# Strassen-style expert layers on one core: the first block's second layer takes the other token half first, later blocks keep totals

## The chip, the cores and the metric

The kernel runs on one core of one Trainium2 chip. The metric is the device time of one execution in microseconds (us).

## The reference, cut to what matters

```python
def _attn_ref(q, k, v):            # 4 x 8 heads, 576 tokens, head 64
    ...                            # top-32 softmax attention
def _moe_ref(x, w1, w2, w3, w_out):
    a = x @ w1
    b = x @ w2
    return (a * b @ w3) @ w_out
def _moe2_ref(x, w_gate, w1, w2):  # N = 2304 tokens, D = 512, E = 8, F = 1024
    logits = x @ w_gate
    P = np.exp(logits - logits.max())
    for _ in range(8):             # rows, then columns, are normed
        ...
    for e in range(E):
        h = np.maximum(x @ w1[e], 0.0)
        out += P[:, e:e + 1] * (h @ w2[e])
    return out
```

The three follow each other. The change touches only the last one, `_moe2_ref`.

## The kernel before, in words

**Number format.** Every fp32 operand of a product is split into a high part in TensorE's fp32r format (ScalarE writes it) and a low part, which is the operand less its high part (VectorE or GpSimd subtracts). A product is then three matmuls: high by high, high by low, low by high.

**Blocks and units.** The expert layer takes 768 tokens (`TB`) at a time, so it has three blocks, s = 0, 1, 2. In a block it walks through 32 units (`NW`), n = 4e + u: expert e and a quarter u of the 1024 hidden columns (two slices of 128). The first layer of a unit is a 2 by 2 Winograd product: seven passes (functions `i0` to `i6`, in the order `CH` of products 6, 1, 4, 2, 0, 3, 5). A pass is a call of `prod`: six matmuls of 384 columns at L1141 into a PSUM bank (A, B or C of the unit; the pool has four), and behind it the sums that Winograd's scheme wants (VectorE, L1156, L1159, or L1352 in the later blocks). All engines work through the program's order, each its own instructions in turn.

**Block 0.** The function `l1` returns the seven passes. Its `relu(i, h, src)` writes for hidden slice i and token half h the high part `hh` (ScalarE, L1163) and right behind it the low part `hl` (VectorE, L1164, which needs the high part). The calls are (0,0) in pass 2, (1,1) in pass 4, (1,0) in pass 5 and (0,1) in pass 6, so half 0 is whole after pass 5 and half 1 after pass 6. The second layer is not Winograd: `l2(n, i)` makes token tile i (0 to 2 in half 0, 3 to 5 in half 1) with six matmuls of 512 columns at L1197 into one of three banks, and VectorE adds it to `acc` (L1208; L1204 for the first expert). The main loop puts one `l2` of the unit before behind each of the passes 1 to 6:

```python
for i, fn in enumerate(ops):
    fn()
    if n and i:
        l2(n - 1, (i + 2) % NTB)
```

so tiles come in the order 3, 4, 5, 0, 1, 2. Behind that the slot splits a weight tile of the next unit (`w_split`: ScalarE L966, GpSimd L967), makes a sum of weights of the unit after it (`w_sums`, VectorE L956, in passes 3 to 6), and takes a step of side work from a list (`slot`: first the norming of P, later the tokens of blocks 2 and 1). In pass 3 the second layer's weights are split (`w2_split`, GpSimd L983). On even u, `w2_more` also makes the seven Winograd weights of the second layer and keeps them in DRAM for the later blocks (VectorE L1001, ScalarE L1005, GpSimd L1006).

**Blocks 1 and 2.** Here the second layer is Winograd too, and it is fed by the gated hidden `h`, of which `d1` writes seven combinations (`parts`: high on ScalarE L1358, low on VectorE or GpSimd L1359). For a pair of units, `group(pair, k, j)` makes product k for output half j with six matmuls of 384 columns at L1413 in one of the three banks `yps`, and `add_m` adds it to an accumulator `M[k]` (VectorE L1423; in a block's first pair ScalarE copies, L1421). One group stands behind each pass, 14 for a pair. The weights of product k are fetched (`v_fetch`, L1317) or, for odd units of block 1, made from the raw weights `wr` (`v_make`: VectorE L1331, ScalarE L1333, GpSimd L1334).

**A block's end.** The scheme's totals are sums of the products. The table `early` puts ten sums of accumulators into the last two units (`plus`, L1427, VectorE and GpSimd), and `finish` runs the last pair's 14 groups in three chains: a chain keeps its PSUM bank and adds the next product to it, and VectorE reads it between (L1461, L1463). `out_cols` transposes the totals (L1433), copies them and sends them to DRAM (L1445, L1449). Block 1's end is followed by block 2's start, block 2's by nothing.

Of the kernel before, what the change touches and what calls it, by code (L numbers as in the profile page):

```python
# [7 lines left out]
F32 = mybir.dt.float32  # L8
# [4 lines left out]
AF = mybir.ActivationFunctionType  # L13
ALU = mybir.AluOpType
# [4 lines left out]
def kernel(  # L19
# [897 lines left out]
    NW = E * NU  # L917
    NP = NTB * (NSB - 1)
    CH = (6, 1, 4, 2, 0, 3, 5)
    KO = (1, 2, 3, 5, 7, 6, 4)  # L920
    V, G_ = nc.vector, nc.gpsimd
    pT = dram.tile([E, NP, 128], F32, name="pT")
    xk = {c: dram.tile([128, 2, KH, TH], F32, name=f"xk{c}") for c in CH}
# [200 lines left out]
    hs = {}  # L1124
    bn = {}
    ready_ps = {}

    def prod(n, c, bank, first):

# [16 lines left out]
    def l1(n):  # L1146

        t = {}

        def new(nm, shape, dt):  # L1150
            t[nm] = wp.tile(shape, dt, name=nm, tag=nm, bufs=2 if dt == F32R else 1)
            return t[nm]

        def plus(nm, ps, x):
            new(nm, [128, TH], F32)
            nc.vector.tensor_tensor(t[nm], ps, t[x], ALU.add)  # L1156

        def into(ps, x):
            nc.vector.tensor_tensor(ps, ps, t[x], ALU.add)  # L1159
            return ps  # L1160

        def relu(i, h, src):
            nc.scalar.activation(t["hh"][:, i, h], src, AF.Relu)  # L1163
            nc.vector.scalar_tensor_tensor(t["hl"][:, i, h], src, 0.0, t["hh"][:, i, h].bitcast(F32),  # L1164
                                           op0=ALU.max, op1=ALU.subtract)

        def i0():
            new("hh", [128, 2, 2, TH], F32R)
            new("hl", [128, 2, 2, TH], F32R)
# [89 lines left out]
    for n in range(NW):  # L1259
        e, u = units[n][1:]  # L1260
        ops = l1(n)
        nxt = units[n + 1][1:]
        nx2 = units[n + 2][1:]
        if n == 6:
            steps += x_ops(2) + p_steps() + x_ops(1)
        for i, fn in enumerate(ops):
            fn()
            if n and i:
                l2(n - 1, (i + 2) % NTB)
            (w_split if n + 1 < NW else w_fetch)(*nxt, CH[i])  # L1270
            if n + 2 < NW:
                if i == 0:
                    w_load(*nx2)
                if 3 <= i:
                    w_sums(*nx2, part=i - 3)
            if stores:
                stores.pop(0)()
            if more and i != 3:
                more.pop(0)()
            if i == 3:  # L1280
                w2_split(e, u)
                if n + 1 < NW:
# [40 lines left out]
    def v_make(n, k):  # L1323

        e, u = units[n][1:]
        a11, a12, a21, a22 = [wr[:, j, DH * i:DH * i + DH] for i in range(2) for j in range(2)]
        src = {1: a11, 2: a12, 3: a12, 5: wr5, 7: a21, 6: a11, 4: a22}[k]
        sums = {1: ((wr5, a21, a22, ALU.add), (a21, a11, a21, ALU.subtract)),
                2: ((a11, wr5, a11, ALU.subtract),), 3: ((a12, a12, a11, ALU.subtract),)}.get(k, ())
        for dst, x, y, op in sums:  # L1330
            nc.vector.tensor_tensor(dst, x, y, op)  # L1331
        t = wk2[n % 2][k]
        nc.scalar.activation(t[:, 0], src, AF.Copy)  # L1333
        nc.gpsimd.tensor_tensor(t[:, 1], src, t[:, 0].bitcast(F32), ALU.subtract)  # L1334
        keep2(e, u, k, t)

    def v_next(n, k):
        if n < len(units):
            (v_make if n < 2 * NW and n % 2 else v_fetch)(n, k)
            if k == KO[-1] and n % 2 and n + 2 < 2 * NW:  # L1340
                v_load(n + 2)

    def d1(n):

        last_ = (n + 1) % NW == 0
        e = units[n][1]
        h = hset[(n - NW) % 3]
        t = tmp
# [51 lines left out]
        return ([i0, i1, i2, i3, i4, i5, i6],  # L1400
                [j0, lambda: parts(7, t["t3"], G_), lambda: parts(6, t["t2"], V if last_ else G_),
                 lambda: parts(4, t["b21"], V if last_ else G_)])

    def group(pair, k, j, ps=None):

        again = ps is not None
        if not again:
            ps = yps.tile([128, 512], F32, name="y", tag="y")[:, 0:TH]
        q_ = 0
        for n in pair:  # L1410
            h, w = hset[(n - NW) % 3][k], wk2[n % 2][k]
            for a, b in ((0, 0), (0, 1), (1, 0)):
                nc.tensor.matmul(ps, w[:, a, 128 * j:128 * j + 128], h[:, b], start=(q_ == 0 and not again),  # L1413
                                 stop=(q_ == 5), skip_group_check=True)
                q_ += 1
        return ps

    def add_m(pair, k, j):
        ps = group(pair, k, j)
        if pair[0] % NW == 0:  # L1420
            nc.scalar.activation(M[k][:, j], ps, AF.Copy)  # L1421
        else:
            nc.vector.tensor_tensor(M[k][:, j], ps, M[k][:, j], ALU.add)  # L1423

    def plus(x, y, eng):
        for j in range(2):
            eng.tensor_tensor(M[x][:, j], M[x][:, j], M[y][:, j], ALU.add)  # L1427

    def out_cols(s, dh, th, j, y, st, eng=None):

# [20 lines left out]

    def finish(s, pair, late):

        bank = {}

        def run1(k, ch, j, *reads):
            bank[ch, j] = group(pair, k, j, bank.get((ch, j)))
            for x, op in reads:
                m = M[x][:, j]
                if op is None:  # L1460
                    V.tensor_tensor(m, m, bank[ch, j], ALU.subtract)  # L1461
                else:
                    V.tensor_tensor(m, bank[ch, j], m, ALU.add)  # L1463

        def run(k, ch, *reads):
            for j in range(2):
                run1(k, ch, j, *reads)

        run(1, "Z", (6, 1))
        late.pop(0)()  # L1470
        plus(7, 6, V)
        late.pop(0)()
        plus(3, 6, G_)
        run(2, "Z", (2, 1))
        for fn in late:
            fn()
        run(5, "Y", (7, 1))
        plus(4, 6, G_)
        run(3, "Y", (3, 1))
        o = [M[k] for k in (1, 5, 6, 2)]  # L1480
        for j in range(2):
            out_cols(s, 0, 0, j, M[2][:, j], o[0])
        run(7, "X", (3, None))
        run(6, "X", (7, 1), (3, 1))
        out_cols(s, 1, 1, 0, M[7][:, 0], o[1])
        run1(4, "X", 0, (4, 1))
        out_cols(s, 0, 1, 0, M[3][:, 0], o[2])
        out_cols(s, 1, 1, 1, M[7][:, 1], o[1])
        run1(4, "X", 1, (4, 1))
        out_cols(s, 0, 1, 1, M[3][:, 1], o[2])  # L1490
        out_cols(s, 1, 0, 0, M[4][:, 0], o[3], V)
        out_cols(s, 1, 0, 1, M[4][:, 1], o[3], V)

    early = {(-2, 6): (2, 1, G_), (-1, 0): (6, 1, G_), (-1, 1): (3, 5, V), (-1, 3): (4, 7, V), (-1, 4): (7, 5, V)}
    todo2 = []
    late = []
    p_load(1, 0)
    v_load(NW + 1)
    for n in range(NW, len(units)):
        s, e, u = units[n]  # L1500
        lone = n % NW < 2
# [5 lines left out]
        for i, fn in enumerate(ops):  # L1507
# [4 lines left out]
                w_fetch(*units[n + 1][1:], CH[i])  # L1512
            if todo2:
                pair, k, j = todo2.pop(0)
                add_m(pair, k, j)
                if j and pair[1] + 2 < NW * (s + 1):
                    v_next(pair[0] + 2, k)
                    v_next(pair[1] + 2, k)
            elif lone:
                v_next(n, KO[i])  # L1520
            if stores:
                stores.pop(0)()
            if late:
                late.pop(0)()
            x, y, eng = early.get(((n % NW) - NW, i), (0, 0, None))
            if x:
                plus(x, y, eng)
        late = later_
        if (n + 1) % NW == 0:
            finish(s, (n - 1, n), late)  # L1530
# [31 lines left out]
```

## Time and profile before

| | us |
|---|---|
| median of 3 runs | 2364.95 (2359.8 to 2366.29) |
| profiled execution, its time | 2366.93 |
| its span, first to last instruction | 2365.1 |
| block 0 from its first second-layer matmul to its last first-layer pass | 824.85 to 1367.82 |
| blocks 1 and 2, first pass of each | 1377.1 and 1873.6 |

| engine | busy us | share |
|---|---|---|
| TensorE matmul (PE) | 2226.4 | 94% |
| VectorE (DVE) | 1877.6 | 79% |
| GpSimd (POOL) | 1442.4 | 61% |
| ScalarE (ACT) | 1206.7 | 51% |

Matmuls overlap in the pipeline, so a busy PE is read by the distance between the starts of its matmuls and by its idle time. In a waiting row the number behind the name of the releaser is the wait's total, and then how often and the longest. Rows on the timeline give start, duration, engine, line, operation, what is written and read, and in brackets the engine's idle time before it and what ended that.

### The profile page before, as it was taken

What the parts mean: (1) busy time and instruction counts of PE and PEld (TensorE: products, weight loads), DVE (VectorE), ACT (ScalarE), POOL (GpSimd) and SP (SyncE); (2) the same over time, 40 slices, a digit from 0 to 9 for tenths busy, and PEclk for the clock granted to TensorE, in tenths of its full rate; (3) what the DMA queues carried; (4) which work ended last, traced back from release to release, by engine and by line L of the source; (5) the groups of instructions that cost most, each with busy time, mean ns of one, the idle gap of its engine ahead of it and who ended that gap; (6) DMA issues with size and microseconds to landing.
All of it is one profiled execution on the core that took longest, in us unless ns stands there. A gap on an engine that the chain in (4) does not pass through costs nothing.

```text
span 2365.1 us, 42495 instructions
## 1 busy us (share of the span) xinstructions
PE 2226.4 (94%) x13466; PEld 2032.9 (86%) x13466; DVE 1877.6 (79%) x4564; ACT 1206.7 (51%) x2706; POOL 1442.4 (61%) x1687
## 2 busy tenths in 40 slices
PE   5896999999999899999999989999999899999998
PEld 4555898889888787877788889999999899999997
DVE  8999899999995588877787766777777767777777
ACT  7999787787775334343333334443443343333332
POOL 6889776777764345565655546666666544444444
PEclk6997999999999999999999999999999999999999
DMA  6554444544541366686666687888888888787773
GB/s 186 151 148 117 105 113 100 124 108 109 124 97 46 121 214 219 223 291 227 237 230 225 222 278 265 277 274 273 274 277 268 297 280 260 252 260 256 255 258 120
DMA packets 350944, 482.57 MB, mean 204 GB/s; under 512 B 94881, under 2 KB 161025, under 8 KB 350721
## 3 DMA queue, kind: packets, MB, share of 16 engines
q1 hardware_dynamic: 349584, 478.03, 63.6%
q8 instruction: 108, 1.77, 0.3%
q10 hardware_dynamic: 1136, 1.84, 0.2%
q14 instruction: 116, 0.94, 0.1%
HBM read 306.59 MB, written 132.43 MB: 186 GB/s over the span
## 4 chain that ended last, share of the span: by engine, by line
PE 65%; DVE 14%; ACT 5%; POOL 5%; DMA 4%; issue 4%; SPq 2%; POOLq 0%; ACTq 0%; DVEq 0%
PE l1ps L1141 22%; PE y L1413 19%; PE abps L628 7%; PE y L1197 5%; PE x2ps L645 4%; PE sps L289 2%; DVE ws L956 2%; PE tx L427 2%; PE tx L398 2%; DVE hl L1164 1%; DVE tkv L338 1%; DMA ws<-in_moe_w_dram 1%; ACT hh L1163 1%; DVE acc L1208 1%; DVE l1ps L1159 1%
## 5 line engine op out<-in xcount | busy, mean ns | idle before, releaser
L1413 PE MATMUL y<-h,v 128*128 128x384 f32 x2688 | 551.0, 341 | 10.6 <-DVE M L1463 6.2
L1141 PE MATMUL l1ps<-xB,wa 128*128 128x384 f32 x2688 | 542.1, 338 | 9.0 <-DVE tm_u L1352 7.7
L1413 PEld LDWEIGHTS y<-h,v 128*128 128x128 f32 x2688 | 486.1, 190 | 12.5 <-DVE M L1463 7.4
L1141 PEld LDWEIGHTS l1ps<-xB,wa 128*128 128x128 f32 x2688 | 473.6, 188 | 13.6 <-DVE tm_u L1352 10.7
L967 POOL TENSOR_TENSOR wa<-ws,wa 128x256 fp32r<-128x256 f32 x217 | 169.1, 786 | 232.8 <-ACT wa L966 222.5
L1197 PE MATMUL y<-wb,hh 128*128 128x512 f32 x768 | 277.0, 403 | 32.2 <-ACT hh L1163 32.1
L1141 PE MATMUL l1ps<-xAh,wa 128*128 128x384 f32 x896 | 264.7, 342 | 4.1 <-DVE c L1156 2.0
L1359 POOL TENSOR_TENSOR h<-tm_t,h 128x384 fp32r<-128x384 f32 x188 | 192.0, 1031 | 89.7 <-ACT h L1358 85.9
L1423 DVE TENSOR_TENSOR M<-y,M 128x384 f32<-128x384 f32 x392 | 211.4, 551 | 40.8 <-PE y L1413 40.4
L1197 PEld LDWEIGHTS y<-wb,hh 128*128 128x128 f32 x768 | 147.0, 191 | 64.2 <-ACT hh L1163 39.8
L1359 POOL TENSOR_TENSOR h<-tm_b,h 128x384 fp32r<-128x384 f32 x126 | 133.4, 1064 | 97.9 <-ACT h L1358 84.1
L1358 ACT ACTIVATE h<-l1ps 128x384 fp32r<-128x384 f32 x128 | 63.0, 492 | 232.2 <-DVE l1ps L1355 232.2
L1141 PEld LDWEIGHTS l1ps<-xAh,wa 128*128 128x128 f32 x896 | 167.2, 191 | 14.7 <-DVE u L1156 3.9
L315 POOL TENSOR_TENSOR low<-s_sb 128x288 int32<-128x288 int32 x144 | 117.4, 815 | 99.5 <-ACT s_sb L293 97.4
L338 DVE MAX8 tkv<-rest 128x8 f32<-128x288 f32 x432 | 175.0, 446 | 0.0
L289 PE MATMUL sps<-kst,qst 128*128 128x288 f32 x640 | 130.0, 332 | 33.8 <-DVE top L322 31.9
L1197 PE MATMUL y<-wb,hl 128*128 128x512 f32 x384 | 156.5, 408 | 2.1
L1334 POOL TENSOR_TENSOR v<-wr,v 128x256 fp32r<-128x256 f32 x112 | 89.0, 797 | 113.2 <-ACT v L1333 89.8
L1141 PE MATMUL l1ps<-xAl,wa 128*128 128x384 f32 x448 | 151.8, 339 | 0.0
L289 PEld LDWEIGHTS sps<-kst,qst 128*128 128x128 f32 x640 | 100.0, 202 | 57.0 <-DVE top L322 45.4
L1208 DVE SCALAR_TENSOR_TENSOR acc<-y,P,acc 128x512 f32<-128x512 f32 x168 | 124.9, 744 | 23.5 <-PE y L1197 23.2
L1396 POOL TENSOR_TENSOR tm_t<-tm_b,tm_t 128x384 f32<-128x384 f32 x64 | 65.7, 1026 | 124.1 <-DVE tm_t L1392 119.9
(208 smaller groups left out, 5346.3 us busy)
## 6 DMA issues: line engine op xcount, KB each, us to landing
wa<-wk SPq DMA_DIRECT2D x448, 256.0 KB, 3.4
v<-vk SPq DMA_DIRECT2D x336, 256.0 KB, 3.7
wk<-wa SPq DMA_DIRECT2D x224, 256.0 KB, 2.6
vk<-v SPq DMA_DIRECT2D x112, 256.0 KB, 2.7
raw<-in_moe_w_dram SPq DMA_DIRECT2D x32, 512.0 KB, 3.8
ws<-in_moe_w_dram SPq DMA_DIRECT2D x128, 128.0 KB, 2.5
ws<-in_moe_w_dram SPq DMA_DIRECT2D x32, 512.0 KB, 4.5
vk<-sp SPq DMA_DIRECT2D x64, 256.0 KB, 3.1
```

What stands on the lines that cost most here:

```text
L289: nc.tensor.matmul(ps[:, e, 0:SH], lhs, kst[p, part][:, hh, SH * e:SH * e + SH], start=(n == 0), stop=(n == len(terms) - 1))
L315: nc.gpsimd.tensor_tensor(low_sb[st][:, j].bitcast(I32), x[:, 0:SH], x[:, SH:S], ALU.add)
L338: nc.vector.max(vt[:, j, c:c + 8], x[:, j])
L628: nc.tensor.matmul(ps[:, 0:n], lhs, rhs[:, c, 0:n], start=(m == 0), stop=(m == 3 * KD - 1))
L645: nc.tensor.matmul(ps[:, 0:n], W[:, f, 128 * c:128 * c + 128], G[:, f, 0:n], start=(f == 0), stop=(f == FC - 1))
L967: eng.tensor_tensor(t[:, 1], st[:, c], t[:, 0].bitcast(F32), ALU.subtract)
L1141: nc.tensor.matmul(ps, lhs[:, kc], rhs[:, kc], start=(first and k_ == 0), stop=(k_ == 3 * KH - 1), skip_group_check=True)
L1197: nc.tensor.matmul(ps, lhs[:, m, h, o:o + 128], rhs[:, m], start=(k_ == 0), stop=(k_ == 5))
L1208: nc.vector.scalar_tensor_tensor(a, ps, P[:, i, e:e + 1], a, op0=ALU.mult, op1=ALU.add)
L1359: eng.tensor_tensor(h[k][:, 1], src, h[k][:, 0].bitcast(F32), ALU.subtract)
L1413: nc.tensor.matmul(ps, w[:, a, 128 * j:128 * j + 128], h[:, b], start=(q_ == 0 and not again), stop=(q_ == 5), skip_group_check=True)
L1423: nc.vector.tensor_tensor(M[k][:, j], ps, M[k][:, j], ALU.add)
```

## The change

1. Block 0: the second layer takes tile i - 1 behind pass i (order 0 to 5).
2. Low parts made by VectorE (`hl`, and those of `parts(1)` and `parts(2)`) are put on a list and issued behind the slot's second-layer group, so behind VectorE's read of that group.
3. `w2_more` is also called for unit 1; block 1's unit 1 then fetches its weights, and the raw weights of its unit 3 are loaded before the block.
4. Blocks 1 and 2: products go in the order 1, 2, 5, 3, 7, 6, 4, and within a pair the chains Z (1, 2), Y (5, 3) and X (7, 6, 4) go on in their bank, so that `M[k]` holds a running total (M2 holds products 1 and 2, M3 holds 5 and 3, M6 holds 7 and 6, M4 holds 7, 6 and 4).
5. A block's end: the early sums are four, on GpSimd, `finish` has a new order with product 2 last, and the low parts there are made by GpSimd.
6. In `v_make` the weight sums move to products 2, 5 and 3.

```diff
-    KO = (1, 2, 3, 5, 7, 6, 4)
+    KO = (1, 2, 5, 3, 7, 6, 4)
+    CHAIN = {1: "Z", 2: "Z", 5: "Y", 3: "Y", 7: "X", 6: "X", 4: "X"}
...
+    after = []
+
+    def run_after():
+        while after:
+            after.pop(0)()
...
             nc.scalar.activation(t["hh"][:, i, h], src, AF.Relu)
-            nc.vector.scalar_tensor_tensor(t["hl"][:, i, h], src, 0.0, t["hh"][:, i, h].bitcast(F32),
-                                           op0=ALU.max, op1=ALU.subtract)
+            after.append(lambda: nc.vector.scalar_tensor_tensor(
+                t["hl"][:, i, h], src, 0.0, t["hh"][:, i, h].bitcast(F32), op0=ALU.max, op1=ALU.subtract))
...
-                l2(n - 1, (i + 2) % NTB)
+                l2(n - 1, i - 1)
+            run_after()
...
-                if u % 2 == 0:
+                if n % 2 == 0 or n == 1:
                     more = w2_more(e, u)
...
-        sums = {1: ((wr5, a21, a22, ALU.add), (a21, a11, a21, ALU.subtract)),
-                2: ((a11, wr5, a11, ALU.subtract),), 3: ((a12, a12, a11, ALU.subtract),)}.get(k, ())
+        sums = {2: ((wr5, a21, a22, ALU.add), (a21, a11, a21, ALU.subtract)),
+                5: ((a11, wr5, a11, ALU.subtract),), 3: ((a12, a12, a11, ALU.subtract),)}.get(k, ())
...
-            (v_make if n < 2 * NW and n % 2 else v_fetch)(n, k)
-            if k == KO[-1] and n % 2 and n + 2 < 2 * NW:
+            (v_make if NW + 1 < n < 2 * NW and n % 2 else v_fetch)(n, k)
+            if k == KO[-1] and n % 2 and NW + 1 < n < 2 * NW - 2:
                 v_load(n + 2)
...
-            eng.tensor_tensor(h[k][:, 1], src, h[k][:, 0].bitcast(F32), ALU.subtract)
+            low = lambda: eng.tensor_tensor(h[k][:, 1], src, h[k][:, 0].bitcast(F32), ALU.subtract)
+            (after.append if eng is V else lambda f: f())(low)
...
-            parts(5, t["t1"], V if last_ else G_)
+            parts(5, t["t1"], G_)
...
+    def group(pair, k, j, first=False):
+
+        first = first or k in (1, 5, 7)
+        if first:
+            bank[CHAIN[k], j] = yps.tile([128, 512], F32, name="y", tag="y")
+        ps = bank[CHAIN[k], j][:, 0:TH]
...
+    def take(pair, k, j, *dst, first=False):
+        ps = group(pair, k, j, first)
+        for x in dst:
+            m = M[abs(x)][:, j]
+            if x < 0:
+                nc.vector.tensor_tensor(m, m, ps, ALU.subtract)
+            elif pair[0] % NW == 0:
+                nc.scalar.activation(m, ps, AF.Copy)
+            else:
+                nc.vector.tensor_tensor(m, ps, m, ALU.add)
...
+        run(1, 1, 2)
         late.pop(0)()
         plus(3, 6, G_)
+        plus(5, 1, V)
+        run(5, 5)
         for fn in late:
             fn()
...
+        plus(3, 1, V)
+        run(3, 3)
+        plus(4, 1, V)
+        run(7, -3)
+        run(6, 5, 3)
+        out_cols(s, 1, 1, 0, M[5][:, 0], M[7])
+        take(pair, 4, 0, 4)
...
+        take(pair, 2, 0, 2, first=True)
+        out_cols(s, 1, 0, 1, M[4][:, 1], M[1])
+        take(pair, 2, 1, 2, first=True)
+        out_cols(s, 0, 0, 0, M[2][:, 0], M[5])
+        out_cols(s, 0, 0, 1, M[2][:, 1], M[5], V)
...
-    early = {(-2, 6): (2, 1, G_), (-1, 0): (6, 1, G_), (-1, 1): (3, 5, V), (-1, 3): (4, 7, V), (-1, 4): (7, 5, V)}
+    early = {3: (3, 7, G_, ALU.subtract), 5: (5, 6, G_, ALU.add)}
...
-    v_load(NW + 1)
+    v_load(NW + 3)
```

## Rows read from the trace of the kernel before

**Rows 1.** Busy time by stretch: length, engines' busy us, granted clock, DMA share.

```profile
1500.00:1600.00 100.00, 100.00 (x570) 99.73 (x569) 78.83 (x153) 41.41 (x94) 66.78 (x72) 1.00 0.80 272
1840.00:1885.00 45.00, 37.93 (x209) 35.50 (x207) 34.57 (x57) 12.70 (x28) 20.28 (x20) 0.96 0.78 294
2320.00:2365.00 45.00, 34.11 (x182) 32.24 (x180) 32.17 (x50) 8.52 (x19) 17.69 (x16) 0.90 0.27 83
```

**Rows 2.** Who waited for whom in block 0, 824 to 1377 us.

```profile
ACT hh L1163 <- DVE l1ps L1159: 139.2, 63, 3.7
DVE hl L1164 <- ACT hh L1163: 68.6, 117, 2.0
PE y L1197 <- ACT hh L1163: 32.1, 23, 3.6
```

**Rows 3.** Timeline at the turn from one unit of block 0 to the next.

```profile
1285.87 0.39 PE L1197 MATMUL y<-wb,hh 128*128 128x512 f32 x1
...
1287.26 0.34 PE L1141 MATMUL l1ps<-xAh,wa 128*128 128x384 f32 x1
...
1289.28 0.55 DVE L1159 TENSOR_TENSOR l1ps<-l1ps,u 128x384 f32<-128x384 f32 x1
1289.87 0.49 ACT L1163 ACTIVATE hh<-l1ps 128x384 fp32r<-128x384 f32 x1 [2.34 <-DVE l1ps L1159]
...
1290.41 0.50 PE L1197 MATMUL y<-wb,hh 128*128 128x512 f32 x1 [0.91 <-ACT hh L1163]
...
1290.86 0.48 ACT L1172 ACTIVATE p<-l1ps 128x384 f32<-128x384 f32 x1
```

**Rows 4.** Busy time in block 0: the first 11, next 10 and last 10 units.

```profile
824.85:1023.65 198.80, 182.87 (x858) 158.64 (x859) 167.84 (x292) 79.38 (x187) 114.61 (x122) 0.96 0.64 219
1023.65:1203.14 179.49, 164.99 (x782) 142.07 (x781) 141.10 (x221) 69.02 (x167) 109.17 (x116) 0.98 0.72 252
1203.14:1367.82 164.68, 159.62 (x780) 139.73 (x779) 129.45 (x207) 60.92 (x146) 87.69 (x95) 1.00 0.67 227
```

**Rows 5.** VectorE's groups in block 0, 830 to 1367 us: count, busy, mean ns, idle before.

```profile
L956 DVE TENSOR_TENSOR ws<-ws 128x256 f32<-128x256 f32 x116 | 112.3, 968 | 9.2 <-DMA ws<-in_moe_w_dram 7.2 <-POOL wb L983 1.9
L1001 DVE TENSOR_TENSOR sm<-ws 128x256 f32<-128x256 f32 x30 | 21.4, 715 | 0.0
```

**Rows 6.** Timeline of block 1's start.

```profile
1388.41 2.35 DVE L1331 TENSOR_TENSOR wr<-wr 128x256 f32<-128x256 f32 x2
...
1391.29 2.35 PE L1141 MATMUL l1ps<-xB,wa 128*128 128x384 f32 x12 [2.65 <-DVE tm_u L1352]
...
1407.39 1.43 DVE L1331 TENSOR_TENSOR wr<-wr 128x256 f32<-128x256 f32 x2 [6.80 <-DMA wr<-in_moe_w_dram]
...
1410.93 2.29 PE L1141 MATMUL l1ps<-xB,wa 128*128 128x384 f32 x6 [3.66 <-DVE tm_u L1352]
```

**Rows 7.** Timeline of block 2's start.

```profile
1885.53 5.60 PE L1141 MATMUL l1ps<-xB,wa 128*128 128x384 f32 x30 [0.37 <-DVE tm_u L1352]
```

**Rows 8.** Timeline of block 2's end.

```profile
2332.34 2.27 PE L1413 MATMUL y<-h,v 128*128 128x384 f32 x12
...
2336.65 1.34 PE L1413 MATMUL y<-h,v 128*128 128x384 f32 x6 [2.04 <-DVE M L1423]
...
2338.18 0.55 DVE L1393 TENSOR_TENSOR tm_t<-tm_b,l1ps 128x384 f32<-128x384 f32 x1
...
2340.82 2.63 DVE L1427 TENSOR_TENSOR M<-M,M 128x384 f32<-128x384 f32 x2
...
2358.65 0.52 PE L1433 MATMUL otp<-ident,M 128*128 128x128 f32 x3 [0.16 <-DVE M L1463]
...
2361.29 0.55 SPq L1449 DMA_DIRECT2D out_dram<-M  x1
```

**Rows 9.** Timeline of block 1 in its steady run: groups and VectorE's reads.

```profile
1506.02 1.22 PE L1413 MATMUL y<-h,v 128*128 128x384 f32 x6
...
1510.01 1.01 DVE L1423 TENSOR_TENSOR M<-y,M 128x384 f32<-128x384 f32 x2
```

More of the change, by code (lines that the diff above doesn't have):

```diff
@@ L1338, in v_next @@
         if n < len(units):
-            (v_make if n < 2 * NW and n % 2 else v_fetch)(n, k)
-            if k == KO[-1] and n % 2 and n + 2 < 2 * NW:
+            (v_make if NW + 1 < n < 2 * NW and n % 2 else v_fetch)(n, k)
+            if k == KO[-1] and n % 2 and NW + 1 < n < 2 * NW - 2:
                 v_load(n + 2)
     def d1(n):
-        last_ = (n + 1) % NW == 0
         e = units[n][1]
@@ L1397, in j0 @@
             G_.tensor_tensor(t["b21"], t["b21"], t["t2"], ALU.subtract)
-            parts(5, t["t1"], V if last_ else G_)
+            parts(5, t["t1"], G_)
         return ([i0, i1, i2, i3, i4, i5, i6],
[L1401 to L1408, printed above, removed]
+                [j0, lambda: parts(7, t["t3"], G_), lambda: parts(6, t["t2"], G_),
+                 lambda: parts(4, t["b21"], G_)])
+    bank = {}
+    def group(pair, k, j, first=False):
[3 more added lines that the diff above has]
+        ps = bank[CHAIN[k], j][:, 0:TH]
         q_ = 0
@@ L1412, in group @@
             for a, b in ((0, 0), (0, 1), (1, 0)):
-                nc.tensor.matmul(ps, w[:, a, 128 * j:128 * j + 128], h[:, b], start=(q_ == 0 and not again),
+                nc.tensor.matmul(ps, w[:, a, 128 * j:128 * j + 128], h[:, b], start=(first and q_ == 0),
                                  stop=(q_ == 5), skip_group_check=True)
@@ L1416, in group, with plus @@
         return ps
[L1418 to L1425, printed above, removed]
+    def take(pair, k, j, *dst, first=False):
[8 more added lines that the diff above has]
+                nc.vector.tensor_tensor(m, ps, m, ALU.add)
+    def plus(x, y, eng, op=ALU.add):
         for j in range(2):
-            eng.tensor_tensor(M[x][:, j], M[x][:, j], M[y][:, j], ALU.add)
+            eng.tensor_tensor(M[x][:, j], M[x][:, j], M[y][:, j], op)
     def out_cols(s, dh, th, j, y, st, eng=None):
@@ L1452, in finish, with run @@
     def finish(s, pair, late):
[L1454 to L1465, printed above, removed]
+        def run(k, *dst):
             for j in range(2):
[L1467 to L1471, printed above, removed]
+                take(pair, k, j, *dst)
+        run(1, 1, 2)
         late.pop(0)()
         plus(3, 6, G_)
-        run(2, "Z", (2, 1))
+        plus(5, 1, V)
+        run(5, 5)
         for fn in late:
             fn()
[L1477 to L1492, printed above, removed]
-    early = {(-2, 6): (2, 1, G_), (-1, 0): (6, 1, G_), (-1, 1): (3, 5, V), (-1, 3): (4, 7, V), (-1, 4): (7, 5, V)}
+        plus(3, 1, V)
[5 more added lines that the diff above has]
+        take(pair, 4, 0, 4)
+        out_cols(s, 0, 1, 0, M[3][:, 0], M[6])
+        out_cols(s, 1, 1, 1, M[5][:, 1], M[7])
+        take(pair, 4, 1, 4)
+        out_cols(s, 0, 1, 1, M[3][:, 1], M[6])
+        out_cols(s, 1, 0, 0, M[4][:, 0], M[1])
+        take(pair, 2, 0, 2, first=True)
[4 more added lines that the diff above has]
+    early = {3: (3, 7, G_, ALU.subtract), 5: (5, 6, G_, ALU.add)}
     todo2 = []
@@ L1514 @@
                 pair, k, j = todo2.pop(0)
-                add_m(pair, k, j)
+                take(pair, k, j, k)
                 if j and pair[1] + 2 < NW * (s + 1):
@@ L1520 @@
                 v_next(n, KO[i])
+            run_after()
             if stores:
@@ L1524 @@
                 late.pop(0)()
-            x, y, eng = early.get(((n % NW) - NW, i), (0, 0, None))
-            if x:
-                plus(x, y, eng)
+            if (n + 1) % NW == 0 and i in early:
+                plus(*early[i])
         late = later_
```

## The prediction

> **What bounds the kernel now.** I read the busy time by stretch first, because a share over the whole span hides that the three blocks have different limits. In the steady run of blocks 1 and 2 TensorE is never idle: 570 matmuls in 100 us at the full granted clock, 2.4 GHz [rows 1]. That is 0.175 us a matmul, 1.05 us for a pass or a group of six, 2.1 us for a slot. No other engine is full there, so an edit that only shifts VectorE's work inside this stretch is worth nothing. What is left is where TensorE stops: 45 us around block 1's end hold 37.9 us of matmuls and 45 us at the end of the program 34.1, at mean clocks of 0.96 and 0.90 [rows 1].
>
> Then I read who waits for whom in block 0. TensorE's largest wait there, 32.1 us in 23 pieces, is a second-layer matmul that waits for a high part of the hidden [rows 2]. The timeline at one such turn shows the mechanism [rows 3]. The last second-layer group of the old unit ends at 1287.26; passes 0 and 1 of the next unit follow (2.1 us) and then the first group, which reads half 1. That half needs the product of pass 6. VectorE adds its sum only at 1289.28, some 3.2 us after the product was there (pass 6 ended where the last group began, 1285.87), ScalarE's high part starts at 1289.87 and TensorE at 1290.41. So VectorE is late, and the kernel reads its latest result first.
>
> The busy time of three stretches of block 0 tells how much can come back [rows 4]. A unit has 42 first-layer matmuls at 0.175 us [rows 1] and 36 second-layer ones at 1.39/6 = 0.232 us [rows 3]: 7.4 + 8.3 = 15.7 us. The 11, 10 and 10 units would take TensorE 172.7, 157 and 157 us; they took 198.8, 179.5 and 164.7. The excess is 26.1, 22.5 and 7.7, together 56 us, idle time and the matmuls at half clock behind it (0.96, 0.98, 1.00 [rows 4]). VectorE was busy for 167.8, 141.1 and 129.5 us [rows 4]. **In the first stretch VectorE has nearly as much work as TensorE**, and this caps the gain.
>
> **Block 0: tile order and late low parts.** The new order reads half 0 first. Its last part comes from pass 5, a pass and a group earlier (1.05 + 1.39 = 2.4 us), and the new low part's place costs one read of a group. The 0.91 us wait [rows 3], and most of the 23, which average 1.4 us, are within that. Tile 3, the first of half 1, comes three slots later, so the part from pass 6 is never urgent again.
>
> The late low parts also free VectorE. Now it stands idle in 117 places for 68.6 us, 0.59 us each, for a high part that ScalarE is just writing [rows 2]. Behind the change it reads the finished group in that time. Where it is behind TensorE, it idles for neither. Where it is not, it waits for the group instead, which costs TensorE nothing.
>
> What is late next? Behind the late high part ScalarE does two short weight splits and then the copy `p`, which the next unit's pass 2 needs. At the shown turn `p` ends at 1290.86 + 0.48 = 1291.34 [rows 3]. Without the wait, TensorE would want it after passes 0 and 1 and one group: 1287.26 + 2.1 + 1.39 = 1290.75. If the 0.59 us that VectorE no longer idles is passed on, `p` ends at 1290.75 too: nothing to 0.6 us is left on each second unit, of which I take 0.3.
>
> Last stretch: 157 + 5 x 0.3 = 158.5, so 6 us come back. First stretch: unit 1's additional weights are four sums of about 0.7 us [rows 5], so VectorE needs 167.8 + 2.6 = 170.4. I add one idle piece of 0.59 us to each of the 11 units (177) and 3 us for units with more work than their neighbours: 180, so 19 us come back. Second stretch: VectorE's mean leaves room, but the token sums of the later blocks lie in single units; I take 5.5 us over TensorE's 157, between the other two, so 17 us. For the first wait, before 824.85, 1 us. **Sum for block 0: 43 us**; from below about 22 (the first two stretches give back only a third of their excess and the last all but 2), from above 56.
>
> The other work of unit 1 (four ScalarE and GpSimd pieces, seven stores) falls on engines that are at most 61% busy in the stretch [rows 4]; block 1 does without the same work. `w_sums` is issued as before; its waits for DMA were 7.2 us in all [rows 5].
>
> Here a rule speaks against the change. The weight sums take 0.97 us in the mean [rows 5], and I let this mean stand. The Trainium skill (SBUF — State Buffer, section Who interferes with whom) says that a VectorE instruction with two SBUF inputs contends with a GpSimd instruction that reads SBUF, and that the later one is fully blocked. A denser block has more such meetings. By that rule the weight sums could grow with the density, 10% on 112 us, an estimate, which would make the sum of block 0 some 5 us smaller; by the rows it stays.
>
> **Blocks 1 and 2 in steady run.** The number of groups, reads and matmuls is the same, and TensorE is full: 0 us. The cover is its queue. It is gone if a chained group finds its bank not yet read, which is the slower rival below. The weight sums in `v_make` leave product 1, where VectorE now stands 6.80 us before them for the raw weights [rows 6].
>
> **Block 1's start.** Making unit 1's weights in the middle of the lone first units blocks VectorE twice: 2.35 us of sums, after which TensorE has waited 2.65 us, and the 6.80 us wait for the raw weights, after which it has waited 3.66 [rows 6]. With the clock lost behind the second one, the excess over 0.175 us a matmul between 1377 and 1420 is 11 us. Block 2 starts with fetched weights, as block 1 now will; its longest wait is 0.37 us [rows 7] and its excess about 1.4. I take 8.5 us back, from 5 to 10.
>
> **The two ends.** From the end of the last pass (about 2333.4: two sixes of 1.05 us from 2332.34, the first being the pass) to the last transposes at 2358.65 [rows 8] are 25.3 us. TensorE's own work there is 15 groups of 1.05 us and eight transposes of about 0.45, 19.4 us. The chain in front is VectorE's: its last difference comes at 2338.18, 4.8 us after the pass, behind early sums that take 1.2 us each where GpSimd runs beside them, and two sums in `finish` take 2.63 us [rows 8]. After the change VectorE has no early sums, so this difference comes about 2.3 us after the pass. But then the totals of products 1 and 2 need four reads at once, the sum into M5 must come before the first read of product 5, and product 3 goes on in the same bank: adding 0.55 us a read and 1.3 a contended sum, product 3 starts about 2 us late. The low parts on GpSimd come late for product 5 by about 1 us, and the X chain waits about 2 us more. I get 19.4 + 5 = 24.4 us, against 25.3: 1 us back, with 0.5 for the waits in front. At the very end the last transfer waits now for three others that are issued before it until 2361.29 [rows 8]; in the new order the outputs lie further apart, 1.3 us. **Ends: 1.5 + 2.8 = 4.3 us**, from -4 to 10.
>
> **Sum.** 43 + 8.5 + 4.3 = 56 us from the profiled execution's 2366.9, 2 us over the median: 2311, or 2309 on the median's scale. I forecast **2310**.
>
> **The rivals.**
> *VectorE becomes the bound of block 0 (0.16).* For: 170.4 us of work in a stretch where TensorE needs 172.7 [rows 4]. If its idle time stays at half of the 68.6 us [rows 2], the first two stretches give back 18 us instead of 36: about 2328, up to 2340 if the ends give nothing. Against: the last stretch has 27 us to spare.
> *All the excess goes (0.12).* 56 + 10 + 8: about 2293.
> *Slower: the running totals stall TensorE (0.04).* Before, a bank is written again after three groups; now product 2 goes into product 1's bank two slots later. The group that starts at 1506.02 is read by the first of the two instructions at 1510.01, till about 1510.5 [rows 9]; two slots later TensorE is at 1506.02 + 4.2 = 1510.2. This read would be 0.3 us too late; most of its neighbours end sooner. Eight groups of 14 are chained, 240 in the 30 pairs of the two blocks: if each waited 0.27 us in the mean, 65 us would be lost and the change would be slower, from 2375 upwards. The Trainium skill (PSUM — Partial Sum Buffer, section PSUM bank collisions raise a hardware error) asks that engines be kept apart on a bank by semaphores, so TensorE has to wait for that read. Against: the reads that come late are those behind VectorE's waits for raw weights and high parts, and both of these go.
> *No measurable change (0.02).* A measurement of this kernel tells about 0.3%, 7 us, from nothing. It would need the wait to return at `p` in full.
>
> The forecast itself, 2300 to 2324, has 0.66. The range reaches to the middle of the neighbours: 2293 to 2334. Faster: 0.66 + 0.16 + 0.12 = 0.94.
>
> **What would show it.** Right: in block 0 no second-layer matmul waits for `hh`, units of 15.7 to 16.5 us, what waiting is left stands at first-layer matmuls behind `p` or VectorE; block 1's start without waits over 0.5 us; 570 matmuls in 100 us in the steady runs. Wrong: idle VectorE time before `acc` of the old size, waits of second-layer matmuls for reads of `M`, or ends longer than 26 us.

## The result and the profile after

The changed kernel takes 2339.91 us in the median (2338.47 to 2342.62, 4 runs) against 2362.51 us before (2359.8 to 2366.29, 4 runs): a ratio of 0.9905, with a 95% interval of 0.9884 to 0.9925. The direction was right and the size was not: 22.6 us came back where 56 were forecast, and the time lies above the range. The two profiled executions differ by 28.4 us of span (2365.1 and 2336.7), since the profiled execution of before took 2366.93 us, more than any of the four timed runs. The split by stretch below is made between these two.

| stretch, by the starts of matmuls | before | after | forecast | measured |
|---|---|---|---|---|
| start of the span to block 1's first pass | 1377.13 | 1357.58 | -43 | -19.6 |
| block 1, first pass to last pass | 468.3 | 464.8 | -8.5 | -3.5 |
| block 1's end, last pass to last transposes | 27.9 | 27.5 | -1.5 | -0.4 |
| block 2 to its last pass | 457.8 | 458.3 | 0 | +0.5 |
| block 2's end | 27.5 | 24.0 | -1.5 | -3.5 |
| from the last transposes to the span's end | 6.5 | 4.6 | -1.3 | -1.9 |

So most of the error lies in block 0, 23.4 us of 27.4. Its busy time first, by units 1 to 11, 12 to 21 and 22 to 31, each stretch from the start of one first second-layer matmul to another. The third ends before the last unit's own second layer, so it is two passes (2.1 us) short of ten whole units. Columns are those of [rows 1]. The borders in [rows 4] lay up to 4 us off the units' true starts, so here is the kernel before with the right ones:

```profile
824.85:1027.82 202.97, 186.03 (x874) 161.31 (x875) 170.90 (x297) 81.13 (x192) 116.32 (x124) 0.96 0.64 218
1027.82:1206.15 178.33, 164.84 (x782) 142.23 (x782) 140.27 (x221) 68.50 (x167) 108.20 (x115) 0.98 0.73 254
1206.15:1368.97 162.82, 157.76 (x770) 137.84 (x770) 127.83 (x204) 60.19 (x144) 86.94 (x94) 1.00 0.66 225
```

and the changed kernel:

```profile
821.15:1018.30 197.15, 181.21 (x875) 157.13 (x875) 177.18 (x303) 83.25 (x198) 123.42 (x130) 0.98 0.68 234
1018.30:1192.49 174.19, 162.13 (x782) 140.28 (x782) 146.35 (x224) 69.32 (x168) 111.99 (x117) 0.99 0.75 262
1192.49:1349.42 156.93, 155.88 (x770) 137.71 (x770) 132.18 (x202) 60.34 (x143) 89.10 (x94) 1.00 0.69 235
```

The last ten units came out as forecast: 156.9 us and the two missing passes are 159.0, where 158.5 were forecast. The first 11 were to fall to 180 and took 197.2, the next ten to 162.5 and took 174.2. VectorE's busy time, the third pair, did not stay: over the 31 units it grew from 439.0 to 455.7 us with seven instructions more (729 instead of 722).

The waits of block 0 (824 to 1360 us) of the changed kernel, which answer to [rows 2]: total, times, longest.

```profile
ACT hh L1169 <- DVE l1ps L1165: 126.8, 63, 3.7
...
DVE acc L1214 <- PE y L1203: 42.9, 54, 2.0
...
PE l1ps L1147 <- ACT p L1178: 16.2, 19, 2.9
...
PE l1ps L1147 <- DVE u L1162: 7.1, 6, 2.0
...
DVE hl L1170 <- ACT hh L1169: 6.7, 7, 2.5
```

No second-layer matmul waits for a high part any more: the 32.1 us of [rows 2] are gone. In their place TensorE waits 16.2 us for the copy `p` and 7.1 for VectorE's `u`. VectorE's own waits for the high part went from 68.6 to 6.7 us, but those for a finished group, 22.6 us in the same view of before, are now 42.9:

```profile
DVE acc L1208 <- PE y L1197: 22.6, 40, 0.8
```

A turn in the first stretch, on the timeline, which answers to [rows 3]:

```profile
860.46 0.96 DVE L1002 TENSOR_TENSOR sm<-sm,ws 128x256 f32<-128x256 f32 x1
...
861.34 0.55 DVE L1165 TENSOR_TENSOR l1ps<-l1ps,u 128x384 f32<-128x384 f32 x1
...
861.93 0.49 ACT L1169 ACTIVATE hh<-l1ps 128x384 fp32r<-128x384 f32 x1 [2.19 <-DVE l1ps L1165]
862.32 0.41 ACT L967 ACTIVATE wa<-ws 128x256 fp32r<-128x256 f32 x1
...
862.62 0.41 ACT L1006 ACTIVATE sp<-sm 128x256 fp32r<-128x256 f32 x1
...
862.93 0.48 ACT L1178 ACTIVATE p<-l1ps 128x384 f32<-128x384 f32 x1
...
863.46 0.44 PE L1147 MATMUL l1ps<-xAh,wa 128*128 128x384 f32 x1 [1.79 <-ACT p L1178]
```

ScalarE stands 2.19 us before the high part of pass 6, which nobody wants before slot 4 of the next unit. Two short instructions and `p` queue behind it, and `p` is what TensorE wants now. VectorE is late here as it was there: its sum for pass 6 starts at 861.34, 3.5 us after TensorE began the next unit (857.79), where the turn of [rows 3] had 2.0.

Why it has no less to do is seen in its groups of block 0 (826 to 1346 us), which answer to [rows 5]: count, busy, mean ns, idle before.

```profile
L957 DVE TENSOR_TENSOR ws<-ws 128x256 f32<-128x256 f32 x117 | 122.0, 1042 | 17.3 <-DMA ws<-in_moe_w_dram 15.7 <-POOL wa L968 1.5
...
L1002 DVE TENSOR_TENSOR sm<-ws,sm 128x256 f32<-128x256 f32 x17 | 16.6, 976 | 0.0
```

The weight sums grew from 968 to 1042 ns in the mean. The sums of the second layer's weights (L1001 before, L1002 now) moved both ways: the kind shown grew from 521 to 976, a second kind (`sm<-sm,ws`) from 663 to 893, and the commonest (`sm<-ws`) fell from 715 to 660. The row of before:

```profile
L1001 DVE TENSOR_TENSOR sm<-ws,sm 128x256 f32<-128x256 f32 x15 | 7.8, 521 | 0.0
```

Outside block 0: the start of block 1 (timeline of TensorE) has lost the two long waits of [rows 6].

```profile
1363.49 5.70 PE L1147 MATMUL l1ps<-xB,wa 128*128 128x384 f32 x30 [0.53 <-DVE tm_u L1358]
1370.23 5.95 PE L1147 MATMUL l1ps<-xB,wa 128*128 128x384 f32 x29 [1.04 <-DVE tm_u L1358]
```

The excess over 0.175 us a matmul between the first pass and 1420 fell from 11 to 2.8 us. But the steady run behind it, to 1780, now has about 5 us more of excess than before. One such place:

```profile
1533.87 0.42 ACT L1340 ACTIVATE v<-wr 128x256 fp32r<-128x256 f32 x1 [6.65 <-DMA wr<-in_moe_w_dram]
...
1535.49 0.56 DVE L1365 TENSOR_TENSOR h<-l1ps,h 128x384 fp32r<-128x384 f32 x1 [3.34 <-ACT tm_b L1378]
...
1536.57 1.32 PE L1147 MATMUL l1ps<-xB,wa 128*128 128x384 f32 x6 [0.80 <-DVE tm_u L1358]
```

ScalarE waits 6.65 us for the raw weights, VectorE's late low part waits 3.34 us for ScalarE, and TensorE in the end 0.80 for VectorE.

At block 1's end the wait that answers to [rows 8] is one for a low part that GpSimd makes:

```profile
1826.40 1.97 POOL L1441 TENSOR_TENSOR M<-M,M 128x384 f32<-128x384 f32 x2
1828.34 0.71 POOL L1341 TENSOR_TENSOR v<-wr,v 128x256 fp32r<-128x256 f32 x1
...
1829.02 1.30 POOL L1403 TENSOR_TENSOR tm_t<-tm_b,tm_t 128x384 f32<-128x384 f32 x1
...
1832.60 10.30 PE L1423 MATMUL y<-h,v 128*128 128x384 f32 x44 [4.71 <-POOL h L1365]
```

The early sums and a weight split stand in front of the difference that product 5 waits for. At block 2's end, without weight splits, this wait is 1.3 us.

### The profile page after: what moved, and what is told of

Read it like the earlier page. It is cut to its first block, busy times and chain, and to the rows that moved or that the text cites. A ratio compares the mean times of both kernels' runs of the same rounds, so it can differ in the third digit from the quotient of the medians.

```text
span 2336.7 us, 42305 instructions
## 1 busy us (share of the span) xinstructions
PE 2217.1 (95%) x13466; PEld 2021.8 (87%) x13466; DVE 1881.6 (81%) x4556; ACT 1193.7 (51%) x2705; POOL 1444.1 (62%) x1686
## 4 chain that ended last, share of the span: by engine, by line
PE 44%; DVE 4%; DMA 2%; issue 1%; POOL 1%; ACT 1%; SPq 0%; ACTq 0%; DVEq 0%; POOLq 0%
PE l1ps L1147 21%; PE y L1423 19%; PE y L1203 3%; DMA wr<-in_moe_w_dram 1%; DVE ws L957 1%; DMA ws<-in_moe_w_dram 1%; DVE acc L1214 0%; DVE sm L1002 0%; DVE l1ps L1361 0%; ACT h L1364 0%; DVE h L1365 0%; DVE hl L1170 0%; POOL wa L968 0%; DVE l1ps L1165 0%; DVE l1ps L1358 0%
## 5 line engine op out<-in xcount | busy, mean ns | idle before, releaser
L1437 DVE TENSOR_TENSOR M<-y,M 128x384 f32<-128x384 f32 x424 | 229.8, 553 | 79.9 <-PE y L1423 79.3
L1147 PE MATMUL l1ps<-xAh,wa 128*128 128x384 f32 x896 | 266.3, 344 | 27.9 <-ACT p L1178 16.2
L1365 POOL TENSOR_TENSOR h<-tm_t,h 128x384 fp32r<-128x384 f32 x192 | 197.8, 1045 | 51.2 <-ACT h L1364 51.2
L1364 ACT ACTIVATE h<-tm_b 128x384 fp32r<-128x384 f32 x128 | 67.1, 524 | 188.2 <-DVE tm_b L1361 182.1
L1214 DVE SCALAR_TENSOR_TENSOR acc<-y,P,acc 128x512 f32<-128x512 f32 x168 | 123.7, 742 | 47.6 <-PE y L1203 42.9
L1341 POOL TENSOR_TENSOR v<-wr,v 128x256 fp32r<-128x256 f32 x105 | 80.3, 765 | 129.2 <-ACT v L1340 114.4
```

What stands on the lines that cost most here:

```text
L1147: nc.tensor.matmul(ps, lhs[:, kc], rhs[:, kc], start=(first and k_ == 0), stop=(k_ == 3 * KH - 1), skip_group_check=True)
L1214: nc.vector.scalar_tensor_tensor(a, ps, P[:, i, e:e + 1], a, op0=ALU.mult, op1=ALU.add)
L1365: low = lambda: eng.tensor_tensor(h[k][:, 1], src, h[k][:, 0].bitcast(F32), ALU.subtract)
L1437: nc.vector.tensor_tensor(m, ps, m, ALU.add)
```

## The experiments

Theory 1: the gain of block 0 is lost on ScalarE's queue, where `p` stands behind the late high part of pass 6. Theory 2, the rival: VectorE's time is the bound; what it no longer idles is eaten by its instructions growing beside GpSimd's. All ratios are to the kernel before, timed on the same chip.

| kernel | median us | ratio (95% interval) | block 1's first pass, us |
|---|---|---|---|
| before | 2361 to 2362.5 | 1 | 1377.1 |
| changed | 2339.91 | 0.9905 (0.9884 to 0.9925) | 1357.6 |
| tile order, low parts at once | 2350.36 | 0.995 (0.9931 to 0.997) | 1368.4 |
| late low parts, old tile order | 2342.52 | 0.9919 (0.9895 to 0.9943) | 1361.3 |
| high part behind `p` | 2316.09 | 0.9806 (0.9784 to 0.9828) | 1337.3 |
| GpSimd writes zeros | 2305.42 | 0.9757 (0.9739 to 0.9775) | 1324.5 |
| ends' low parts on VectorE | 2337.22 | 0.9897 (0.9882 to 0.9911) | 1355.9 |
| block 0's edits alone | 2343.30 | 0.9929 (0.9912 to 0.9946) | 1354.0 |
| behind `p`, ends on VectorE | 2319.99 | 0.9823 (0.9809 to 0.9838) | 1340.7 |
| block 1's sums at product 1 | 2333.66 | 0.9882 (0.9867 to 0.9897) | 1355.1 |
| behind `p`, sums levelled | 2311.98 | 0.9792 (0.9772 to 0.9811) | 1333.3 |
| behind `p`, zeros | 2297.96 | 0.9729 (0.971 to 0.9748) | 1318.3 |
| behind `p`, low parts at once | 2324.52 | 0.9844 (0.9828 to 0.9859) | 1343.7 |
| behind `p`, levelled, sums at product 1 | 2306.51 | 0.9771 (0.9753 to 0.9789) | 1329.0 |

**The tile order without the late low parts.**

```diff
-            after.append(lambda: nc.vector.scalar_tensor_tensor(
-                t["hl"][:, i, h], src, 0.0, ...
+            nc.vector.scalar_tensor_tensor(t["hl"][:, i, h], src, 0.0, ...
```

> The changed kernel, but block 0's low parts are made right behind their high parts again, so of block 0's edits only the tile order (and unit 1's weights) stays. Theory 1 (the gain is lost on ScalarE's queue: the copy p stands behind the late high part of pass 6): the tile order alone carries little, because VectorE's waits for the high part are back and the late sum of pass 6 is as late as before: p waits of 20 to 30 us instead of 16, 2346 to 2354 us. Theory 2 (VectorE's time is the bound and contention eats what it saves): VectorE idles 0.59 us for each high part again, all of it comes back as time in the first 21 units: 2350 to 2360 us. If the late low parts were worth nothing: 2340.

2350.36 us: in the band that both theories share. Its waits in block 0 (824 to 1340 us) show both causes at once, VectorE's idle time for high parts nearly back at its old size, 0.58 us a piece, and more waiting for `p`:

```profile
DVE hl L1170 <- ACT hh L1169: 58.5, 101, 2.6
...
PE l1ps L1147 <- ACT p L1178: 21.5, 19, 3.0
```

**The late low parts without the tile order.**

```diff
-                l2(n - 1, i - 1)
+                l2(n - 1, (i + 2) % NTB)
```

> The changed kernel with the old tile order 3, 4, 5, 0, 1, 2 in block 0; the low parts stay late. Both theories: the first group still reads the part of pass 6, whose low part now comes behind one more read, so the waits for hh or hl return at 1 to 2 us a unit: 2355 to 2370 us. If the late low parts alone carried the gain: 2340 to 2345.

2342.52 us, far under what I expected and in the band for late low parts that carry the gain alone. It is 2.6 us from the changed kernel, inside the intervals of both. The late low parts alone carry nearly the whole gain; the order alone carried 11 us (2361.5 to 2350.36), so the two gains overlap. The waits for the high part did come back, as expected, but they cost little more than the waits for `p` that stand there with the new order (same view and window):

```profile
DVE acc L1214 <- PE y L1203: 40.8, 54, 1.9
...
PE y L1203 <- ACT hh L1169: 20.0, 20, 2.2
```

**The high part of pass 6 behind the copy `p`.**

```diff
+        def i6():
+            ps = into(prod(n, 5, "C", False), "u2")
+            held.append(lambda: relu(0, 1, ps))
...
             nc.scalar.activation(new("p1", [128, TH], F32), ps, AF.Copy)
+            while held:
+                held.pop(0)()
```

> The changed kernel, but the high part of pass 6 (half 1, not wanted before slot 4 of the next unit) is issued on ScalarE behind the next unit's copy p, and its low part behind that. Nothing else moves. Theory 1 (ScalarE's queue): TensorE's 16 us of waits for p and the half-clock matmuls behind them go, 2315 to 2325 us, and block 0's first 21 units fall from 17.5 to 16.5 us or less. Theory 2 (VectorE is the bound): TensorE then waits for VectorE's u, c and sums at the same places, 2332 to 2340 us.

2316.09 us: theory 1's band, 24 us under the changed kernel for one high part a unit (its low part goes with it) in another place of the queue; 20 of them lie before block 1's first pass. TensorE's waits of block 0 (824 to 1340 us), and the busy time of the three stretches:

```profile
PE l1ps L1148 <- DVE u L1163: 13.4, 13, 2.6
```

```profile
820.51:1008.82 188.31, 178.36 (x876) 156.89 (x875) 169.79 (x302) 82.64 (x196) 123.43 (x130) 0.99 0.71 245
1008.82:1175.25 166.43, 158.48 (x782) 139.60 (x782) 142.23 (x224) 69.28 (x168) 113.49 (x117) 1.00 0.79 274
1175.25:1329.16 153.91, 153.91 (x769) 138.31 (x769) 127.72 (x201) 60.20 (x143) 88.59 (x93) 1.00 0.70 240
```

In the third stretch TensorE never stops: its nine whole units (1175.25 to 1315.65) take 15.60 us each, which is TensorE's own time (the forecast had used 15.7). The first 21 units still take 354.7 us, 16.9 a unit, where 21 x 15.60 would be 327.6 and theory 1 had asked for 16.5. There the waits now stand at VectorE's `u`. By TensorE's own time the three stretches would be 481.5 us; the changed kernel is 46.8 over that and this one 27.1. Theory 1 explains 20 of the excess, not all of it, and even these not cleanly: waits for `p` fell from 16.2 to 0.7 us, but VectorE's busy time fell too, from 455.7 to 439.8, with nearly the same instructions. In its groups (830 to 1330 us) some sums are short again:

```profile
L957 DVE TENSOR_TENSOR ws<-ws 128x256 f32<-128x256 f32 x115 | 117.5, 1022 | 12.4 <-DMA ws<-in_moe_w_dram 9.3 <-POOL wb L984 1.9 <-POOL wa L968 1.1
...
L1002 DVE TENSOR_TENSOR sm<-ws,sm 128x256 f32<-128x256 f32 x16 | 9.1, 566 | 0.0
```

So the sums do not simply grow with the density of the schedule: block 0 is 20 us shorter here than in the changed kernel. How much of the 20 us comes from the shorter sums no run separates.

**GpSimd writes zeros instead of subtracting.**

```diff
+        if eng is nc.gpsimd:
+            nc.gpsimd.memset(t[:, 1].bitcast(F32), 0.0)
+        else:
             eng.tensor_tensor(t[:, 1], st[:, c], t[:, 0].bitcast(F32), ALU.subtract)
```

> The changed kernel, but in block 0 GpSimd writes zeros into the low parts of the first layer's weights instead of subtracting, so it reads nothing from SBUF there (this leaves the low part of these weights out of the result). Theory 2 with contention as its cause: VectorE's weight sums fall from 1042 ns in the mean to 700 or less, some 40 us of VectorE's time, and the program takes 2305 to 2320 us. If the sums are long for another reason they stay at 950 ns or more and the time within 5 us of 2340. Theory 1 alone says nothing on the sums.

2305.42 us, at the low edge of theory 2's band. VectorE's weight sums shrank without an edit to them, in its groups of 830 to 1340 us:

```profile
L957 DVE TENSOR_TENSOR ws<-ws 128x256 f32<-128x256 f32 x115 | 87.6, 761 | 9.3 <-DMA ws<-in_moe_w_dram 9.2
```

761 ns instead of 1042, not quite the 700 I had set as the mark; other GpSimd instructions that read are still there. So part of VectorE's time is time beside GpSimd's reads. The Trainium skill (SBUF — State Buffer, section Who interferes with whom) says that a VectorE instruction with two SBUF inputs contends with a GpSimd instruction that reads SBUF and not with one that only writes it: this run agrees, 1042 against 761 ns. In its trace the 56 weight sums that met no read of GpSimd's took 0.42 us in the mean, 13 of them beside such a write; the 60 that met a read took 1.08. The edit also shortens GpSimd's own work, and ScalarE's waits for it (17.7 us in 11 places) go too. Such waits alone need not cost time: behind `p` they are 21.9 us and the third stretch still has TensorE full.

**Both, queue and zeros.**

> The high part of pass 6 behind p, and GpSimd writes zeros as the low parts of the first layer's weights in block 0 (left out of the result). If queue and contention are two separate losses, every unit runs at TensorE's 15.6 us and the program takes 2288 to 2297 us. If they are the same loss seen twice, it takes what the zeros alone took: 2303 to 2306.

2297.96 us, 1 us over the band for two separate losses. Busy time of the three stretches:

```profile
821.08:999.05 177.97, 175.02 (x875) 156.10 (x875) 158.71 (x304) 84.14 (x199) 83.75 (x131) 1.00 0.77 261
999.05:1156.27 157.22, 156.37 (x783) 140.33 (x783) 124.89 (x220) 68.83 (x166) 73.80 (x114) 1.00 0.84 289
1156.27:1310.18 153.91, 153.91 (x770) 138.31 (x770) 119.36 (x201) 61.69 (x143) 57.34 (x92) 1.00 0.70 236
```

7.6 us over TensorE's own time are left of the changed kernel's 46.8, at a granted clock of 1.00 throughout. The two losses overlap (24 and 34 us singly, 42 together): a VectorE that is earlier also lets the high part of pass 6 off ScalarE's queue sooner. With the zeros alone, and the queue as it was, the wait for `p` is down from 16.2 us (824 to 1340 us):

```profile
PE l1ps L1150 <- ACT p L1181: 3.7, 4, 1.7
```

**The order and the queue, without the late low parts.** The edit is those of the first and the third run together.

> The high part of pass 6 behind p, but block 0's low parts are made right behind their high parts, as before the change. If ScalarE's queue is the whole of what the tile order needed, the late low parts add nothing any more: 2314 to 2320 us. If VectorE's time counts too, its 0.59 us of idle time for each high part comes back in the first 21 units: 2326 to 2340.

2324.52 us, between the two bands. Without the late low parts the repair of the queue gives 26 us (from 2350.36), and the late low parts add 8 on top. Only with the repair does the tile order pay more than a few us beside the late low parts.

**Two weight sums of block 0 to passes with less work.**

```diff
-                if 3 <= i:
+                if i in (3, 4):
                     w_sums(*nx2, part=i - 3)
+            if 0 < n < NW - 1 and i in (0, 2):
+                w_sums(*nxt, part=2 + i // 2)
```

> The kernel with the high part of pass 6 behind p, and two of the four weight sums that VectorE makes in passes 3 to 6 of a unit of block 0 moved to passes 0 and 2 of the next unit, where it has less to do. The number of instructions is the same. If what is left of the waits comes from VectorE's work being bunched in passes 3 to 6 (late by up to 3 us at pass 6), 5 to 12 us more come back against the kernel with the high part moved alone (2316): 2304 to 2311 us. If VectorE's total in the first 21 units is the bound, the place of the sums changes nothing: 2314 to 2319.

2311.98 us, 4 under the kernel with the queue repaired and between the two bands; the intervals overlap (0.9772 to 0.9811 and 0.9784 to 0.9828). The first 11 units fell from 188.3 to 183.3 us, the next ten stayed at 166.4 and 166.6. Bunching is at most a part of the remainder.

**The ends' low parts on VectorE again.** Parts 5, 6 and 4 of a block's last unit go to VectorE, alone and with the queue repaired.

> The changed kernel, but in a block's last unit the low parts for products 5, 6 and 4 are made by VectorE again, as before the change. If GpSimd's queue is what makes product 5 wait at the ends (4.7 us at block 1's end, 1.3 at block 2's, and the half clock behind them), 4 to 7 us come back: 2333 to 2336 us. If VectorE's chain of reads and sums is the limit there, VectorE only gets three more instructions: 2339 to 2343 us.

> Both repairs: the high part of pass 6 behind the next unit's copy p, and the ends' low parts on VectorE. If they add up: 24 us from the first and 4 to 7 from the second, 2308 to 2313 us. If the second is worth nothing: 2316.

Alone 2337.22 us, between the two bands and inside the changed kernel's interval; block 1's end took 27.3 us instead of 27.5 and block 2's 24.6 instead of 24.0. With the repair 2319.99, not under 2316.09; the ends took 25.8 and 26.2 us. The wait for GpSimd was real, but VectorE's chain of reads and sums beside it ends no earlier: at block 1's end of the first run TensorE waits 1.63 us for VectorE's low part and 1.36 for its sum instead. This theory of mine fell: the ends are not improved by giving the low parts back.

**Block 0's edits alone.**

> The kernel before with the tile order and the late low parts of block 0 alone (no weights of unit 1 ahead, later blocks and ends as before). By the account of the traces the block 0 part is worth about 20 us and the rest 8 to 9: 2340 to 2346 us. If the later blocks' edits are worth nothing in the sum: 2337 to 2340. If they carry most: over 2350.

2343.30 us, as the account of the traces had it: block 0's edits are worth 17 to 18 us in the medians (0.9929), all the rest about 3, less than the 8.8 that the two profiled executions show outside block 0. Its profile shows one price that the change pays inside block 0: the first 11 units take 193.6 us here, and 197.0 to 197.5 in the three profiled kernels with the same block 0 and unit 1's weights (the changed one and the two with an edit only behind block 0). Unit 1's weights cost about 3.5 us there.

**Block 1's weight sums with product 1.**

> The changed kernel with the weight sums of block 1 issued with product 1 again instead of 2 and 5. If the sums' new place causes the 5 us that block 1's steady run lost (VectorE's u3 late behind them), that run is at 0.175 us a matmul again: 2335 us. If VectorE's wait for the raw weights (up to 6.8 us at product 1) now meets banks that are written again sooner, waits of second-layer matmuls for M appear and it gets slower: 2342 to 2360 us.

> The high part of pass 6 behind p, the levelled weight sums of block 0, and block 1's weight sums with product 1 again. If all add up: 3 to 5 us under the kernel without the last edit, 2300 to 2308 us.

2333.66 us alone, near the 2335 expected, though the interval overlaps that of the changed kernel. The steady run of block 1, from its first group to its last pass, took 442.6 us here and 442.4 in the second run, 2306.51 us, which has all three edits (queue, levelled sums, sums at product 1) and lies in its band. With the sums at products 2 and 5 the other ten profiled kernels with the new later blocks took 442.7 to 446.5 us, 445.3 in the mean, so a single pair of runs does not settle it: about 3 us, if anything. At 0.175 us a matmul it would be 437.9, so the sums' place is not the whole of the excess. No waits of second-layer matmuls for M appeared. The second run is the fastest that leaves nothing out, 2.3% under the kernel before and 1.4% under the changed one.

## Why the prediction was wrong

**What bounds the kernel: right.** Block 2 ran as before with TensorE full (571 matmuls in 100 us), and most of the time came from block 0.

**Tile order: the step that failed is "What is late next?".** It had the right instruction and the wrong size. I took 0.3 us for the wait for `p` on each second unit, 1.5 us in the last ten units, and left it out of the sum for the others. Measured were 16.2 us of waits for `p` in 19 places. The last ten units have four of them, of 0.25 to 0.3 us, as forecast; the other 15 us stand in the units that had no such term. Putting `p` in front gave 24 us, and block 0 then gives back 39.8 us (1377.1 to 1337.3) of the 43 forecast. The rows of before had it: in [rows 3] the high part ends at 1290.36 and `p` at 1291.34, 0.98 us behind it, and the new deadline is only one group, 1.39 us, behind the old. So the new order moved the deadline by 1.39 us and put 0.98 us of queue in front of it: 0.4 us net, not the 2.4 us that I set against the wait. The run with the old tile order, 2.6 us slower than the changed kernel, agrees with this.

That the last ten units came out within 0.5 us is in part luck. TensorE's own unit is 15.60 us and not 15.7, and each second unit took 16.3 to 16.4, 0.7 more and not 0.3; the two misses cancel.

**Late low parts: the mechanism was right, the size half.** I let VectorE's 68.6 us of idle time go and added only one 0.59 us piece a unit. The idle time for high parts did go (6.7 us left). But 20 us more were spent waiting for groups, and 16.7 us more on work: 455.7 instead of 439.0 us, most of it longer instructions; unit 1's four sums, forecast at 2.6, are a part. The first 21 units, forecast at 180 + 162.5, took 197.2 + 174.2.

**Contention with GpSimd's reads was set at 5 us and kept out of the sum.** The weight sums grew 8% (968 to 1042 ns), near the 10% of that estimate, but other sums moved too, one kind by 87%. The reason given, density, does not hold: behind `p`, in a still denser block 0, VectorE's busy time is that of before. Which instructions meet, and when, is what changed: of the sums of that kind 11 of 16 met no read of GpSimd's before, and 1 of 17 in the changed kernel. The prediction had no term for this. What it costs where VectorE has no time to spare shows in the run with zeros: VectorE was busy for 410.2 instead of 455.7 us, and the 31 units took 31.1 us less. How much of the 23 us missing in block 0 is contention and how much is queue can't be split, since the two overlap: without the queue's loss the first 21 units are at 354.7 us, without contention's 343.2, without both 335.2, where TensorE's own time is 327.6.

**The rival with VectorE as the bound** (0.16, 2328 and up to 2340) is the nearest to what happened, in its place and its price; it lacked the queue. I gave it too little, because I held the totals of work against each other and not the order in one turn.

**Block 1's start: right in its place, then in part given back.** 8.2 of the 8.5 us came back between the first pass and 1420, though waits of 0.53 and 1.04 us were left where none over 0.5 was forecast; about 5 were lost again in the steady run that I had set at 0, and 3.5 had been paid in block 0 for unit 1's weights. One place of the loss is shown (raw weights, ScalarE, late low part, `u3`). Whether the late low parts or the new place of the sums brought it was not settled.

**The ends: right in the sum** (-4.3 forecast, -5.8 measured), by luck, for the parts were not: block 1's end gave 0.4 us, block 2's 5.4 with its tail. At block 1's end TensorE waited 4.7 us for product 5's low part on GpSimd, where I had counted about 1; but with that low part on VectorE the end was as long, so what bounds it stays open. A reading was wrong as well: the two sixes from 2332.34 in [rows 8] are groups (L1413) and the last pass ended where they start, so the end of before was 26.3 us long for the 15 groups counted, not 25.3.

**The running totals did not stall TensorE.** The slower rival's sign, waits of second-layer matmuls for reads of M, is 1.6 us in all in blocks 1 and 2 of the changed kernel, none of it in the steady runs.

## What to carry to other kernels

When an order change makes one operand less urgent, look what stands behind its producer in that engine's queue: an instruction that is no longer urgent but still waits blocks the urgent one behind it. Moving it back, which only the reordering allows, gave 24 us here; the reordering before that had given 3 on top of the late low parts. Set the new deadline against the new late item on one turn of the timeline, in full, before taking the difference of the old ones as the gain. And where two engines share reads, what one of them saves in idle time is not all free time: how long its instructions take depends on which of the other's they meet, and a new order can change that either way. A mean read before the change need not hold behind it.

## What the runs showed of the hardware that I had not expected

The mean of VectorE's 128 x 256 weight sums, the same instructions each time, was 968 ns before, 1042 in the changed kernel, 1022 with the high part behind `p`, and 761 when GpSimd wrote zeros in place of a subtraction. In all four traces such a sum took 0.41 to 0.43 us where no read of GpSimd's overlapped it. A unit of block 0 with nothing in TensorE's way takes 15.60 us for 78 matmuls, within 1% of what I had put together from single groups.
